# Moving the operand sums of a second matrix product between the blocks of an interleaved schedule

## The chip, the cores and the metric

One core of a Trainium2 chip runs the whole program. The metric is the device time of one execution in microseconds (us). The kernel before was run three times: 297.32, 300.2 and 303.18 us, median 300.2. Changes of about 2% are the smallest that a comparison here is meant to tell from none.

## The reference, cut to what matters

A linear attention (softmax over the head dimension of q, softmax over the sequence of k, then two small products) is followed by a two-layer network with SiLU. Its output has 4608 rows, and nearly all of the arithmetic is in the two layers:

```python
kv = np.einsum('bhsd,bhse->bhde', k_s, v)
attn = np.einsum('bhsd,bhde->bhse', q_s, kv)      # 8 batches, 8 heads, 576 rows, 64 wide
x = attn.transpose(0, 2, 1, 3).reshape(4608, 512)
h = x @ w_in                                       # 512 -> 2048
g = h * (1.0 / (1.0 + np.exp(-h)))
out = g @ w_out                                    # 2048 -> 512, float32
```

## The kernel before, in words

The 4608 rows are cut into nine chunks of 512 (chunk 0 to chunk 8). For each chunk the kernel needs its slice of the attention output (XT, 512 wide, transposed), the first product with W1 and SiLU (result GT, two buffers GT0 and GT1 that chunks use in turn), and the second product with W2.

From chunk 1 on, the second product is done in the manner of Strassen and Winograd: the 2048x512 weight W2 and the chunk's GT are cut into two by two blocks, and seven block products P1 to P7 replace eight. The price is sums on VectorE (DVE). On the weight side there are T1 to T4, made once (`t_op`, line 439; T3 is written over a quarter of W2, T4 has two halves). On the data side there are S1 to S4, made for every chunk (`s_op`, line 429): S1 = GT01 + GT11, S2 = S1 - GT00, S3 = GT00 - GT01, which is written in place over GT01, and S4 = GT10 - S2. P5 uses S1 and T1, P6 uses S2 and T2, P7 uses S3 and T3, P4 uses T4, and P3 uses S4. P1 and P2 need no sum. Half of the first product is done in the same way (`group`, lines 344 to 382, matmuls on line 357; its sums on line 320 are called XS here); the other half is plain (`mm1`, matmuls on line 274).

The order of the work is written out by hand. The list `units` holds small blocks of work, and `plan(u, f)` puts extra work in front of unit u. All instructions are issued in that order, each engine runs its own in order, and engines wait for each other through semaphores. `begin[t]` is the first unit of chunk t. For t = 2 to 7 a chunk has 29 blocks: 15 that alternate a plain first-product matmul group of chunk t (`p`) with half of a block product of chunk t-1 (`b`), and then 14 that mix the seven Strassen groups of chunk t (`g`) with the remaining halves (`b`). The products come in the order 1, 2, 6, 5, 7, 4, 3, two halves each:

```python
mix = "pbpbpbpbpbpbpbp", "ggbgbgbgbbgbgb"
```

So P7 begins in block 19, P4 in block 23 and P3 in block 26. In chunk 8 the two parts stand the other way round: there P7 begins in block 17, P4 in block 21 and P3 in block 25.

PSUM sets the coupling around the change. Banks 0 to 3 hold the plain groups `p` in turn. Each is emptied by two instructions: ScalarE (ACT) takes the tanh (line 246, into one of three buffers sg), then DVE multiplies (line 247, scalar_tensor_tensor, into GT). The first two Strassen groups, g1 and g2 in blocks 15 and 16, take over banks 0, 1 and banks 2, 3. So the matmuls of g1 and g2 can't start before DVE has emptied these banks of the last `p` groups. From chunk 3 on the eighth `p` is in bank 0; in chunk 2 it is in bank 2, with the sixth in bank 0 and the seventh in bank 1.

Besides, DVE adds up rows of the exponentials of q for the next batch (line 144) and takes their reciprocals (line 148); GpSimd (POOL) scales the exponentials with these (line 153) and casts v (line 91, into vaug); kv (line 185) and the attention product (line 224) follow in the second part of a chunk. DVE also combines the Strassen results (line 336 for the first product, lines 475 and 486 for the output tiles ow). In chunk 7 and 8 no batch is left to prepare, and POOL has nothing of this to do.

Of the kernel before, what the change touches and what calls it, by code (L numbers as in the profile page):

```python
# [17 lines left out]
def kernel(  # L18
# [9 lines left out]
    nc = tc.nc  # L28
# [257 lines left out]
    def mm1(t, fb):  # L286
        bank = hb[0] % hb[1]
        hb[0] += 1
        mm1_mm(t, fb, bank, range(NC))
        mm1_silu(t, fb, bank)  # L290
# [22 lines left out]
    def xs_op(t, i):  # L313
        in0, in1 = {
            1: (xb(t, 0, 1), xb(t, 0, 0)),
            2: (xb(t, 1, 1), XS4[0]),
            3: (xb(t, 1, 1), xb(t, 0, 1)),
            4: (xb(t, 1, 0), XS4[1]),
        }[i]
        nc.vector.tensor_tensor(out=XS4[i - 1], in0=in0, in1=in1, op=ALU.subtract)  # L320
# [23 lines left out]
    def group(t, i):  # L344
        bank = 0 if i in (1, 6, 7, 4) else 2
        a, bb = {
            1: (wa(0, F0), xb(t, 0, 0)),
            2: (wa(1, F0), xb(t, 1, 0)),
            3: (WS[3], xb(t, 1, 1)),
            4: (wa(1, F1), XS4[3]),  # L350
            5: (WS[0], XS4[0]),
            6: (WS[1], XS4[1]),
            7: (WS[2], XS4[2]),
        }[i]
        for p in range(4):
            for c in range(2):
                nc.tensor.matmul(  # L357
                    out=PS[:, bank + p // 2, (p % 2) * HT:(p % 2 + 1) * HT],
                    lhsT=a[:, c, p * 128:(p + 1) * 128],
                    rhs=bb[:, c, :],  # L360
                    start=(i in (1, 2, 5) and c == 0 and p % 2 == 0),
                    stop=(i in (2, 3, 4) and c == 1 and p % 2 == 1),
                    skip_group_check=True,
                )
        if i == 1:
            group_snap(0)
        elif i == 2:
            group_add(0)
        elif i == 6:
            group_snap(1)  # L370
            group_silu(t, 0, F0, 0)
        elif i == 7:
            group_snap(2)
            group_add(2)
        elif i == 4:
            group_silu(t, None, F1, 0)
        elif i == 3:
            group_silu(t, 2, F1, 1)
            group_add(1)
            group_silu(t, 1, F0, 1)  # L380
# [36 lines left out]
    def blk(t, kh, th):  # L417
        return GTS[t % 2][:, kh * HF:(kh + 1) * HF, th * HT:(th + 1) * HT]

    def s_op(t, i, f0=0, f1=HF):  # L420
        in0, in1, op = {
            1: (blk(t, 0, 1), blk(t, 1, 1), ALU.add),
            2: (SS[1], blk(t, 0, 0), ALU.subtract),
            3: (blk(t, 0, 0), blk(t, 0, 1), ALU.subtract),
            4: (blk(t, 1, 0), SS[2], ALU.subtract),
        }[i]
        f = slice(f0, f1)
        o = blk(t, 0, 1) if i == 3 else SS[i]
        nc.vector.tensor_tensor(out=o[:, f], in0=in0[:, f], in1=in1[:, f], op=op)  # L429

    def t_op(i, eng, f0=0, f1=HF):
        o, in0, in1 = {
            1: (T1, B12, B11),
            2: (T2, B22, T1),
            3: (T3, B22, B12),
            4: (T4, B21, T2),
        }[i]
        f = slice(f0, f1)
        eng.tensor_tensor(out=o[:, f], in0=in0[:, f], in1=in1[:, f], op=ALU.subtract)
# [160 lines left out]
    def plan(u, f):  # L600
        at.setdefault(u, []).append(f)
# [7 lines left out]
    begin = {1: len(units)}  # L609
# [6 lines left out]
    def b_units(t, order):  # L616
        got = []
        for i in order:
            got.append(lambda t=t, i=i: prod(t, i, 0))

            def second(t=t, i=i):
                prod(t, i, 1)
                after(t, i)

            got.append(second)
        return got
# [8 lines left out]
    for t in range(2, NCH):  # L635
        begin[t] = len(units)
        bs = b_units(t - 1, ORDER)
        ps_ = [lambda t=t, fb=fb: mm1(t, fb) for fb in (0, 8, 1, 9, 2, 10, 3, 11)]
        gs = [lambda t=t, i=i: group(t, i) for i in (1, 2, 6, 5, 7, 4, 3)]
        plan(begin[t] + 2, lambda t=t: s_op(t - 1, 1))  # L640
        plan(begin[t] + 4, lambda t=t: s_op(t - 1, 2))
        plan(begin[t] + 11, lambda t=t: s_op(t - 1, 3))
        plan(begin[t] + 16, lambda t=t: s_op(t - 1, 4))
        mix = "pbpbpbpbpbpbpbp", "ggbgbgbgbbgbgb"
        for x in "".join(mix) if t < NCH - 1 else "ggbgbgbgbbgbgb" + "pbpbpbpbpbpbpbp":
            units.append({"p": ps_, "b": bs, "g": gs}[x].pop(0))
        assert not (ps_ or bs or gs)
        x = begin[t] + (1 if t < NCH - 1 else 0)
        plan(x, lambda t=t: (xs_op(t, 1), xs_op(t, 2), xs_op(t, 3), xs_op(t, 4)))
# [102 lines left out]
    plan(b1 + 30, lambda: mm2_plain_out(0, (2, 3)))  # L752
    plan(begin[2], lambda: (hb.__setitem__(0, 3), hb.__setitem__(1, 4)))
    plan(begin[3], lambda: hb.__setitem__(0, 1))
    plan(begin[2] + 12, lambda: t_op(3, nc.vector))
    plan(begin[2] + 14, lambda: t_op(4, nc.vector, 0, 4))
    plan(begin[2] + 16, lambda: t_op(4, nc.vector, 4, 8))

    for t in range(2, NCH - 1):
        b = t + 1  # L760
# [58 lines left out]
```

## Time and profile before

| what | value |
|---|---|
| the three timed runs | 297.32, 300.2, 303.18 us |
| the profiled execution | 300.68 us |
| its span, first to last instruction | 298.9 us |
| mean granted TensorE clock | 0.959 |
| TensorE matmuls (PE), busy | 269.3 us (90%) |
| VectorE (DVE), busy | 206.8 us (69%) |
| ScalarE (ACT), busy | 182.4 us (61%) |
| GpSimd (POOL), busy | 72.1 us (24%) |
| HBM read and written | 36.70 MB and 9.44 MB |

How to read the profile: each row of a timeline is a start, a duration, an engine, the line of the kernel, and out<-in with shapes. Brackets give the engine's idle time before it and what ended that. PE is TensorE's matmuls, PEld its weight loads. PEclk is the clock that TensorE was granted, 1.00 being full speed. The first row of the wait view is a sum over all waits of one kind, then their number, then the longest.

### The profile page before, as it was taken

The page shows a single profiled execution, that of the slowest core. Times are in us where ns is not written, and L with a number is a line of the kernel's source. Part 1 is how long each engine was busy: PE and PEld are TensorE (multiplying, and loading weights), DVE is VectorE, ACT ScalarE, POOL GpSimd, SP SyncE. Part 2 cuts the span into 40 slices and gives each one's busy share as a digit, 9 for nine tenths or more (in the row PEclk, how much of TensorE's full clock was granted, in tenths as well). Part 3 has the DMA queues.
Part 4 walks back from the last instruction along what each step waited for, and adds up shares of the span by engine and source line. Part 5 has one row for each costly group of instructions (what it writes and reads, how often), then busy time and mean ns, then how long its engine had stood idle before and what let it go on. Part 6 is the DMA issues. An engine that isn't in the chain of part 4 may idle for free.

```text
span 298.9 us, 6097 instructions
## 1 busy us (share of the span) xinstructions
PE 269.3 (90%) x2540; PEld 189.4 (63%) x2540; DVE 206.8 (69%) x294; ACT 182.4 (61%) x232; POOL 72.1 (24%) x62
## 2 busy tenths in 40 slices
PE   8799999999499986999599977999599989999994
PEld 3377544456277654776387645866387668886783
DVE  3867888789944897259935896459835964666753
ACT  5768748578347891679457871789267446765320
POOL 0936925402800054000900063002700000000002
PEclk9999999999869996999989997999799999999999
DMA  7999996898661567335782479251403300600343
GB/s 263 293 224 346 286 317 261 206 383 269 164 231 29 113 226 196 132 82 138 197 283 58 87 237 232 86 118 24 79 2 77 66 0 2 136 8 3 78 99 105
DMA packets 35500, 45.88 MB, mean 154 GB/s; under 512 B 16208, under 2 KB 20048, under 8 KB 35472
## 3 DMA queue, kind: packets, MB, share of 16 engines
q1 hardware_dynamic: 29568, 33.69, 40.5%
q0 software_dynamic: 5584, 11.54, 14.8%
q8 instruction: 20, 0.33, 0.5%
q10 hardware_dynamic: 320, 0.26, 0.3%
q14 instruction: 8, 0.07, 0.1%
HBM read 36.70 MB, written 9.44 MB: 154 GB/s over the span
## 4 chain that ended last, share of the span: by engine, by line
PE 56%; DVE 23%; ACT 11%; issue 4%; DMA 2%; POOL 1%; SPq 0%; DVEq 0%; ACTq 0%
PE PS L455 22%; PE PS L357 14%; PE PS L274 11%; DVE GT L247 7%; DVE zq L144 4%; DVE GT L429 4%; PE PS L393 3%; PE PS L254 3%; DMA vt<-in_v_dram 2%; DVE ow L475 2%; ACT L342 2%; PE PS L224 2%; ACT GT L342 2%; ACT sg L246 2%; ACT h L333 2%
## 5 line engine op out<-in xcount | busy, mean ns | idle before, releaser
L247 DVE SCALAR_TENSOR_TENSOR GT<-sg,PS 128x512 f16<-128x512 f32 (+2 forms) x88 | 58.1, 675 | 21.8 <-ACT sg L246 21.0
L274 PE MATMUL PS<-XT,W 128*128 128x512 f16 (+1 forms) x288 | 71.2, 373 | 0.3 <-ACT ow L405 0.3
L246 ACT ACTIVATE sg<-PS 128x512 f32<-128x512 f32 (+2 forms) x88 | 51.7, 597 | 28.7 <-PE PS L274 24.3
L153 POOL TENSOR_TENSOR eq<-eq,rzq 128x1152 bf16<-128x1152 bf16 x13 | 27.5, 2117 | 128.0 <-DVE rzq L148 125.6
L455 PEld LDWEIGHTS <-GT 128*128 128x128 f16 x512 | 49.6, 98 | 13.1 <-issue 1.2
L333 ACT COPY h<-PS 128x1024 f32<-128x1024 f32 x21 | 21.2, 1012 | 47.4 <-PE PS L357 47.4
L455 PE MATMUL PS<-W,GT 128*128 128x256 f16 x384 | 49.1, 273 | 0.0
L455 PEld LDWEIGHTS <-S 128*128 128x128 f16 x384 | 38.8, 101 | 10.1
L336 DVE TENSOR_TENSOR h<-PS,h 128x1024 f32<-128x1024 f32 x21 | 25.7, 1225 | 24.6 <-PE PS L357 20.1
L274 PEld LDWEIGHTS <-W 128*128 128x128 f16 x288 | 27.9, 98 | 21.3 <-issue 1.3
L357 PE MATMUL PS<-XT,W 128*128 128x256 f16 x112 | 19.8, 347 | 20.8 <-DVE GT L247 20.8
L357 PEld LDWEIGHTS <-W 128*128 128x128 f16 x168 | 19.0, 113 | 28.0 <-issue 22.6
L455 PE MATMUL PS<-T,S 128*128 128x256 f16 x256 | 35.3, 286 | 0.0
L475 DVE SCALAR_TENSOR_TENSOR ow<-PS,sc 128x512 f32<-128x512 f32 x7 | 4.8, 692 | 28.9 <-ACT sc L471 28.9
L357 PEld LDWEIGHTS <-WS 128*128 128x128 f16 x224 | 21.7, 101 | 4.5 <-issue 1.2
L342 ACT ACTIVATE GT<-h 128x1024 f16<-128x1024 f32 x21 | 22.2, 1058 | 2.1 <-DVE h L336 2.1
L357 PE MATMUL PS<-XS,WS 128*128 128x256 f16 x168 | 22.8, 281 | 0.0
L89 ACT CAST XT<-PS 128x1024 f16<-128x1024 f32 (+2 forms) x18 | 17.4, 964 | 7.7 <-PE PS L224 7.7
L676 POOL DMA_DIRECT2D out_dram<-ow x4 | 2.2, 550 | 77.8 <-DVE ow L661 77.8
L91 POOL CAST vaug<-vt 128x1152 bf16<-128x1152 f32 x12 | 20.4, 1730 | 0.0
L108 ACT ACTIVATE eq<-qt 128x1152 bf16<-128x1152 f32 x16 | 18.6, 1161 | 2.9 <-DMA qt<-in_q_dram 2.8
L111 ACT ACTIVATE ek<-kt 128x1152 bf16<-128x1152 f32 x16 | 18.7, 1170 | 0.7 <-DMA kt<-in_k_dram 0.7
(76 smaller groups left out, 333.3 us busy)
## 6 DMA issues: line engine op xcount, KB each, us to landing
out_dram<-ow SPq DMA_DIRECT2D x64, 128.0 KB, 2.4
qt<-in_q_dram SPq DMA_DIRECT2D x12, 576.0 KB, 4.9
kt<-in_k_dram SPq DMA_DIRECT2D x12, 576.0 KB, 5.6
vt<-in_v_dram SPq DMA_DIRECT2D x12, 576.0 KB, 6.8
qt<-in_q_dram POOLq DMA_DIRECT2D x4, 576.0 KB, 13.0
kt<-in_k_dram POOLq DMA_DIRECT2D x4, 576.0 KB, 13.3
vt<-in_v_dram POOLq DMA_DIRECT2D x4, 576.0 KB, 12.5
W<-in_moe_w_out_dram POOLq DMA_DIRECT2D x4, 512.0 KB, 15.0
```

Source lines behind the costliest of these rows:

```text
L91: eng.tensor_copy(o, i)
L108: nc.scalar.activation(out=half(st[b]["eq"], cc), in_=jgd(b, "qt", cc), func=ACT.Exp)
L111: nc.scalar.activation(out=half(ek, cc), in_=jgd(b, "kt", cc), func=ACT.Exp)
L153: eng.tensor_tensor(out=e, in0=e, in1=r[:, :, :, None].to_broadcast([128, J, 2, D]), op=ALU.mult)
L246: nc.scalar.activation(out=s, in_=i, func=ACT.Tanh, scale=OS)
L247: nc.vector.scalar_tensor_tensor(out=o, in0=s, scalar=1.0, in1=i, op0=ALU.add, op1=ALU.mult)
L274: nc.tensor.matmul(out=PS[:, bank, o0:TCH], lhsT=W1[:, c, fb * 128:(fb + 1) * 128], rhs=XTS[t % 2][:, c, o0:TCH], start=(c == 0), stop=(c ...
L333: nc.scalar.copy(out=H[i], in_=PS[:, 0:2, :].rearrange("p b n -> p (b n)"))
L336: nc.vector.tensor_tensor(out=H[i], in0=PS[:, 2:4, :].rearrange("p b n -> p (b n)"), in1=H[i], op=ALU.add)
L342: nc.scalar.activation(out=group_out(t, f, n), in_=x, func=ACT.Silu, scale=1.0 / XS)
L357: nc.tensor.matmul(out=PS[:, bank + p // 2, (p % 2) * HT:(p % 2 + 1) * HT], lhsT=a[:, c, p * 128:(p + 1) * 128], rhs=bb[:, c, :], start=(i ...
L455: nc.tensor.matmul(out=PS[:, bank, m * HN:(m + 1) * HN], lhsT=a[:, fc, m * 128:(m + 1) * 128], rhs=bb[:, fc, :], start=(first and fc == 0) ...
```

## The change

Five numbers of the plan change. S3 (`s_op(.., 3)`) moves from block 11 of each chunk to block 5, S4 from block 16 to block 21. In chunk 2, T3 moves from block 12 to block 15, and the two halves of T4 from blocks 14 and 16 to blocks 18 and 20. Nothing is added or taken away; PE's, POOL's and the DMA queues' own orders stay the same, and ACT's too.

```diff
-        plan(begin[t] + 11, lambda t=t: s_op(t - 1, 3))
-        plan(begin[t] + 16, lambda t=t: s_op(t - 1, 4))
+        plan(begin[t] + 5, lambda t=t: s_op(t - 1, 3))
+        plan(begin[t] + 21, lambda t=t: s_op(t - 1, 4))
...
-    plan(begin[2] + 12, lambda: t_op(3, nc.vector))
-    plan(begin[2] + 14, lambda: t_op(4, nc.vector, 0, 4))
-    plan(begin[2] + 16, lambda: t_op(4, nc.vector, 4, 8))
+    plan(begin[2] + 15, lambda: t_op(3, nc.vector))
+    plan(begin[2] + 18, lambda: t_op(4, nc.vector, 0, 4))
+    plan(begin[2] + 20, lambda: t_op(4, nc.vector, 4, 8))
```

DVE's order in chunk 3 before, from S2 (S_78<-S_77,..) to the add that combines g1 and g2 (L336). GT_75 is GT0, which P1 to P7 of chunk 2 read; GT_76 is GT1, which the `p` groups fill; the row GT_75<-GT_75 is S3, S_79 is S4:

```order
L429 TENSOR_TENSOR S_78<-S_77,GT_75 128x2048
L247 SCALAR_TENSOR_TENSOR GT_76<-sg,PS 128x512
L144 TENSOR_REDUCE zq<-eq 128x18
L148 RECIPROCAL rzq<-zq 128x18
L247 SCALAR_TENSOR_TENSOR GT_76<-sg,PS 128x512
L475 SCALAR_TENSOR_TENSOR ow<-PS,sa 128x2x256
L144 TENSOR_REDUCE zq<-eq 128x18
L148 RECIPROCAL rzq<-zq 128x18
L247 SCALAR_TENSOR_TENSOR GT_76<-sg,PS 128x512 x2
L429 TENSOR_TENSOR GT_75<-GT_75 128x8x256
L247 SCALAR_TENSOR_TENSOR GT_76<-sg,PS 128x512 x2
L429 TENSOR_TENSOR S_79<-GT_75,S_78 128x2048
```

The same place now:

```order
L429 TENSOR_TENSOR S_78<-S_77,GT_75 128x2048
L247 SCALAR_TENSOR_TENSOR GT_76<-sg,PS 128x512
L429 TENSOR_TENSOR GT_75<-GT_75 128x8x256
L144 TENSOR_REDUCE zq<-eq 128x18
L148 RECIPROCAL rzq<-zq 128x18
L247 SCALAR_TENSOR_TENSOR GT_76<-sg,PS 128x512
L475 SCALAR_TENSOR_TENSOR ow<-PS,sa 128x2x256
L144 TENSOR_REDUCE zq<-eq 128x18
L148 RECIPROCAL rzq<-zq 128x18
L247 SCALAR_TENSOR_TENSOR GT_76<-sg,PS 128x512 x4
L336 TENSOR_TENSOR h_1511<-PS,h_1511 128x1024
L429 TENSOR_TENSOR S_79<-GT_75,S_78 128x2048
```

S3 now stands ahead of both row sums instead of ahead of the last two multiplies, and S4 behind the add of line 336 instead of ahead of it. S3 is still ahead of the last multiply. Chunks 4 to 6 show the same exchange.

DVE's order in chunk 2 before, from the fifth and sixth multiply to the add of line 336 (W_71<-W_71 is T3, T_74 is T4):

```order
L247 SCALAR_TENSOR_TENSOR GT_75<-sg,PS 128x512 x2
L429 TENSOR_TENSOR GT_76<-GT_76 128x8x256
L439 TENSOR_TENSOR W_71<-W_71 128x8x256
L247 SCALAR_TENSOR_TENSOR GT_75<-sg,PS 128x512
L439 TENSOR_TENSOR T_74<-W_71,T_73 128x1024
L247 SCALAR_TENSOR_TENSOR GT_75<-sg,PS 128x512
L429 TENSOR_TENSOR S_79<-GT_76,S_78 128x2048
L439 TENSOR_TENSOR T_74<-W_71,T_73 128x1024
L336 TENSOR_TENSOR h_1122<-PS,h_1122 128x1024
```

The same place now:

```order
L247 SCALAR_TENSOR_TENSOR GT_75<-sg,PS 128x512 x4
L439 TENSOR_TENSOR W_71<-W_71 128x8x256
L336 TENSOR_TENSOR h_1121<-PS,h_1121 128x1024
L439 TENSOR_TENSOR T_74<-W_71,T_73 128x1024 x2
L429 TENSOR_TENSOR S_79<-GT_76,S_78 128x2048
```

The four sums that stood among the last multiplies and ahead of the add are gone from there: S3 went forward to block 5, the others stand behind the last multiply.

## The prediction

> **What bounds the kernel now.** I read the page first, then the waits of TensorE, then the timeline of PE around those waits.
>
> ```profile
> PE 269.3 (90%) x2540; PEld 189.4 (63%) x2540; DVE 206.8 (69%) x294; ACT 182.4 (61%) x232; POOL 72.1 (24%) x62
> ...
> PE PS L357 <- DVE GT L247: 20.8, 7, 4.0
> ```
>
> PE is the busiest engine, and only one kind of wait of its matmuls is large: seven times, 20.8 us in all, the Strassen groups (L357) wait for DVE's multiply (L247), which empties the banks that they need. The timeline shows these seven: two in chunk 2, then one in each of chunks 3 to 7.
>
> ```profile
> 81.36 1.01 PE L357 MATMUL PS<-XT,W 128*128 128x256 f16 x4 [4.04 <-DVE GT L247]
> 82.92 1.87 PE L357 MATMUL PS<-XT,W 128*128 128x256 f16 x8 [0.55 <-DVE GT L247]
> ...
> 114.89 3.57 PE L357 MATMUL PS<-XT,W 128*128 128x256 f16 x16 [3.69 <-DVE GT L247]
> ...
> 148.79 3.26 PE L357 MATMUL PS<-XT,W 128*128 128x256 f16 x16 [3.69 <-DVE GT L247]
> ...
> 181.13 2.48 PE L357 MATMUL PS<-XT,W 128*128 128x256 f16 x16 [3.69 <-DVE GT L247]
> ...
> 213.79 3.19 PE L357 MATMUL PS<-XT,W 128*128 128x256 f16 x16 [3.69 <-DVE GT L247]
> ...
> 243.78 1.91 PE L357 MATMUL PS<-XT,W 128*128 128x256 f16 x16 [1.41 <-DVE GT L247]
> ```
>
> The same 16 matmuls take 1.91 us in chunk 7, after a short wait, and 2.48 to 3.57 us after the long ones. So the wait costs twice: as idle time, and as slow matmuls behind it. The granted clock, asked for in stretches of 3.4 and 6.8 us, shows why:
>
> ```profile
> 79.91:86.74 6.83, 4.83 (x23) 3.25 (x23) 5.92 (x7) 1.01 (x1) 1.82 (x1) 0.50 1.00 303
> ...
> 114.05:120.87 6.82, 5.98 (x29) 4.12 (x29) 4.00 (x4) 1.01 (x1) 1.71 (x2) 0.50 1.00 272
> ...
> 148.18:151.59 3.41, 2.80 (x14) 1.94 (x14) 2.54 (x2) 0.90 (x1) 1.47 (x2) 0.50 1.06 164
> 178.90:182.31 3.41, 1.18 (x11) 1.06 (x11) 3.41 (x4) 0.11 (x1) 3.10 (x2) 1.00 0.76 152
> 182.31:185.73 3.42, 3.42 (x18) 2.44 (x17) 1.98 (x2) 0.91 (x1) 0.00 (x0) 0.50 0.97 246
> ...
> 213.03:216.45 3.42, 2.66 (x13) 1.86 (x13) 2.70 (x3) 0.76 (x1) 1.63 (x2) 0.50 0.81 154
> 240.35:243.77 3.42, 2.02 (x14) 1.18 (x13) 2.37 (x4) 1.25 (x3) 0.00 (x0) 1.00 0.00 0
> ...
> 175.49:178.90 3.41, 1.95 (x13) 1.17 (x12) 3.38 (x5) 2.19 (x4) 2.82 (x3) 1.00 0.79 266
> ```
>
> The first number behind the length is PE's busy time, the last but two is the clock. In each of chunks 2 to 6 the clock falls to 0.50 for 3.41 us or twice that, and the falls lie whole multiples of 3.41 us apart (79.91 to 114.05 is ten), so they follow a fixed raster. A raster window with 1.18 us of PE work was followed by a slow one; windows with 1.95 and 2.02 us were not. At half clock, half of the busy time is lost: 2.4 us in chunk 2, and 3.0, 1.4, 1.7 and 1.3 us, together 7.4 us, in chunks 3 to 6.
>
> What makes the multiply late is in DVE's timeline of chunk 3 (the first five rows); the sixth row is from chunk 7, the last two are POOL's of chunk 3:
>
> ```profile
> 105.28 0.69 DVE L247 SCALAR_TENSOR_TENSOR GT<-sg,PS 128x512 f16<-128x512 f32 x1
> ...
> 107.52 0.63 DVE L247 SCALAR_TENSOR_TENSOR GT<-sg,PS 128x512 f16<-128x512 f32 x1
> ...
> 110.22 1.22 DVE L247 SCALAR_TENSOR_TENSOR GT<-sg,PS 128x512 f16<-128x512 f32 x2
> 111.35 2.29 DVE L429 TENSOR_TENSOR GT<-GT 128x2048 f16<-128x2048 f16 x1
> 113.57 1.27 DVE L247 SCALAR_TENSOR_TENSOR GT<-sg,PS 128x512 f16<-128x512 f32 x2
> ...
> 240.17 1.22 DVE L429 TENSOR_TENSOR GT<-GT 128x2048 f16<-128x2048 f16 x1
> ...
> 107.74 2.12 POOL L153 TENSOR_TENSOR eq<-eq,rzq 128x1152 bf16<-128x1152 bf16 x1 [26.01 <-DVE rzq L148]
> ...
> 110.45 2.12 POOL L153 TENSOR_TENSOR eq<-eq,rzq 128x1152 bf16<-128x1152 bf16 x1 [0.59 <-ACT ek L111]
> ```
>
> None of the rows of chunk 3, nor any between them, has an idle time in brackets: DVE is full from 105.28 on, and the last multiply, which ends at 114.84, lets g1 start at 114.89. S3 takes 2.29 us here because POOL's scaling runs until 112.57; in chunk 7, with POOL idle, the same sum takes 1.22 us.
>
> **The change part by part.**
>
> S3 in chunks 3 to 6. In block 5 it stands behind the multiply of 105.28, still ahead of the last multiply on an engine that is full between them. So moving it frees nothing by the order alone; all work ahead of the last multiply is the same. What is saved is the price: POOL has been idle for 26.01 us until 107.74, since it waits for the reciprocal that now comes behind S3, so S3 should run at 1.22 instead of 2.29 us. That is 1.07 us a chunk, 4.3 us over four chunks, with both ends between 0 (POOL in its way there too) and 1.07. The wait of 3.69 becomes 2.62 us. The row sums and one multiply shift back by 1.1 us: the fourth multiply, which empties bank 0 for the eighth plain group, and POOL's scaling. Both have cover: the eighth group starts at 110.17, that multiply (107.52) ended at 108.15 and would end at 109.3; and what follows POOL is needed late.
>
> ```profile
> 112.51 3.25 POOL L91 CAST vaug<-vt 128x1152 bf16<-128x1152 f32 x2
> ...
> 124.00 0.80 PE L185 MATMUL PS<-vaug,ek 64*64 64x65 bf16 x72
> 125.39 0.69 DVE L475 SCALAR_TENSOR_TENSOR ow<-PS,sc 128x512 f32<-128x512 f32 x1 [5.59 <-ACT sc L471]
> ...
> 110.17 1.03 PE L274 MATMUL PS<-XT,W 128*128 128x512 f16 x4
> ```
>
> The casts end 8.2 us ahead of the product that reads them. With the casts 1.1 us later and PE up to 4 us earlier, 3 us are left.
>
> S4 in chunks 3 to 7. It moves from in front of the add (L336) to behind it, into the 5.59 us in which DVE waits for ACT. Between 1.22 us and the 2.07 us that it took beside the casts it fits; P3 needs it five blocks later. I take nothing for it. If the cover were gone, the output add, the copy of kv and the attention product behind it would wait with it, 1.2 us a chunk or more.
>
> Chunk 2. Here S3, T3 and half of T4 stood among the last multiplies:
>
> ```profile
> 75.20 1.22 DVE L247 SCALAR_TENSOR_TENSOR GT<-sg,PS 128x512 f16<-128x512 f32 x2
> ...
> 76.33 2.29 DVE L429 TENSOR_TENSOR GT<-GT 128x2048 f16<-128x2048 f16 x1
> ...
> 76.72 0.60 PE L357 MATMUL PS<-XT,W 128*128 128x256 f16 x4
> ...
> 77.49 4.24 POOL L91 CAST vaug<-vt 128x1152 bf16<-128x1152 f32 x2
> ...
> 78.55 2.16 DVE L439 TENSOR_TENSOR W<-W 128x2048 f16<-128x2048 f16 x1
> ...
> 82.19 0.67 DVE L247 SCALAR_TENSOR_TENSOR GT<-sg,PS 128x512 f16<-128x512 f32 x1
> ...
> 87.39 1.04 PE L455 MATMUL PS<-W,GT 128*128 128x256 f16 x8
> ```
>
> With S3 ahead at 1.14 us (1.22 less the overlap with its neighbour), the fifth and sixth multiply end at 77.56, the seventh at 78.2, the eighth at 78.8. The first half of g1, which ran at 76.72, now waits 0.9 us, its second half and g2 0.15 us each: 1.2 us of idle time in place of 4.04 + 0.55. That is 3.4 us saved, and with windows this full the clock has no cause to fall: 2.4 us more, together 5.8. Everything up to P7 (87.39) moves to about 81.5. T3 starts at 78.8, right behind the eighth multiply, while POOL casts; T3 took 2.16 us in that company, which would end at 81.0, just ahead of P7. If it had to let both casts pass (3.25 us from about 78.7), it would end at 83.1 and P7 would wait 1.6 us. I take 0, since one of the two casts was let through in the old row, and keep 1.6 for the range. The Trainium skill speaks against this spot: SBUF — State Buffer, section SBUF: two separate sides, says that a VectorE operation with two SBUF inputs and a GpSimd operation exclude each other for a whole instruction. The trace agrees (2.29 against 1.22 us); by that rule T3 would start at the first cast's end, some 80.3, and end near 81.4, and the sum stays.
>
> Chunks 7 and 8. In chunk 7 the wait of 1.41 us is for the tanh of the last group, not for a full DVE, and S3 costs 1.22 us already: nothing. In chunk 8 PE has no wait; S4 now ends some 0.5 us ahead of P3 there, by the same 1.2 us durations: nothing.
>
> The clock in chunks 3 to 6. An idle stretch of 2.62 us is new. The limit lies between 1.4 and 2.2 us of idle time in one window of 3.41 (1.95 and 1.18 us busy, above). If 2.62 us fall anywhere on the raster, more than 1.4 us of them lie in one window in 9 cases of 10, more than 2.2 in 4 to 5 of 10; I take two thirds to three quarters. So three of four chunks still fall, each for one window at 1.4 us lost (the three single ones lost 1.3 to 1.7): 4.2 us in place of 7.4, a saving of 3.2, between 0 and 7.4.
>
> Sum: 5.8 + 4.3 + 3.2 = 13.3 us. Against the profiled execution of 300.7 us (span 298.9) this gives **287.4 us**; the median of the three runs, 300.2, is the same within their spread.
>
> **The rivals.**
>
> The clock falls in all four chunks as before. The idle stretch stays longer than 2.2 us, which speaks for it. Then 5.8 + 4.3 = 10.1: 290.6 us.
>
> The clock falls in none. Then 5.8 + 4.3 + 7.4 = 17.5: 283.2 us. For it: a wait shorter than one window can never leave a whole window empty. Against it: the window before 182.31 held 1.18 us of work and the clock still fell. The Trainium skill has this rule (TensorE: Matmul & The Clock Gate, section What's actually happening: back to half clock after at least one idle window of about 3.4 us); the trace agrees with the length of the window but not with the need for a wholly idle one.
>
> S3 is still in POOL's way. Then chunks 3 to 6 keep their wait of 3.69 and their clock, and chunk 2 gains 4.7 instead of 5.8 us: 296.0 us, within 2%. Against it: the 26.01 us in which POOL has nothing to run.
>
> Slower: S4 takes the place of the wait. It stands ahead of the output add, the kv copy and the attention product on DVE. If it ended behind the 5.59 us of cover, PE would wait for the attention product; only from 2.7 us beyond the cover in each of five chunks is the gain of 13.3 us used up, and at twice that (5.4 us) the time is 300.7 - 13.3 + 27.0 = 314.4. Against it: the longest S4 in the trace took 2.07 us.
>
> **How the numbers follow.** Forecast, some of the four falls left: 0.5. All falls left: 0.18. None left: 0.17. S3 in POOL's way, or T3 holding P7 on top: 0.1. Slower: 0.02; the rest is spread. The range reaches from 283 (no fall left) to 292.5 (all falls left, and P7 waiting 1.6 us). Faster by over 2% (below 294.2; about 2% is also what a measurement of this kernel can tell from no change): 0.9; within 2%: 0.08; slower: 0.02.
>
> **What would show each step.** Right: the wait of L357 for L247 at about 2.6 us in chunks 3 to 6, under 1 us apiece in chunk 2, and still 1.41 in chunk 7; S3 (GT<-GT) at 1.22 us throughout; stretches at clock 0.50 fewer or shorter; P7, P4 and P3 without a wait. Wrong: S3 still at 2.29 us; the wait gone from L357 but back at L455 (for T3, T4 or S4) or at the attention product; a wait of 2.6 us with all the slow windows as before (then the first rival), or with none (then the second).

## The result and the profile after

The changed kernel takes 286.42 us (median of four runs, 285.22 to 286.89); the kernel before takes 300.69 us beside it (297.32 to 303.18). The ratio is 0.9555, with a 95% interval of 0.9466 to 0.9644: faster. Between the medians it is 14.3 us; the ratio leaves out the kernel before's run of 303.18 us, which is over 1.5% above that kernel's fastest, and stands for some 13.4 us. The forecast was 287.4 us, a gain of 13.3. The profiled execution took 286.77 us, with a span of 285.0 us against 298.9.

The page of the kernel after, its engines, and then the longest of its waits on PE:

```profile
PE 264.4 (93%) x2539; PEld 186.7 (66%) x2540; DVE 197.5 (69%) x294; ACT 182.4 (64%) x232; POOL 66.6 (23%) x62
...
PE PS L357 <- DVE GT L247: 10.1, 6, 2.0
PE PS L455 <- DVE ow L475: 1.9, 4, 0.5
```

The wait of the Strassen groups for the multiply has halved, from 20.8 to 10.1 us. A second wait is new: four times, some half a microsecond, a block product (L455) waits for the output add (L475). PE's busy time fell by 4.9 us though it does the same matmuls, since fewer of them ran at half clock. The same places in PE's timeline as before, chunks 2 to 7:

```profile
76.11 1.03 PE L274 MATMUL PS<-XT,W 128*128 128x512 f16 x4
77.85 2.23 PE L357 MATMUL PS<-XT,W 128*128 128x256 f16 x16 [0.71 <-DVE GT L247]
...
81.67 1.04 PE L455 MATMUL PS<-W,GT 128*128 128x256 f16 x8
...
102.72 1.03 PE L274 MATMUL PS<-XT,W 128*128 128x512 f16 x4
104.21 1.03 PE L455 MATMUL PS<-T,S 128*128 128x256 f16 x8 [0.47 <-DVE ow L475]
105.08 1.03 PE L274 MATMUL PS<-XT,W 128*128 128x512 f16 x4
108.10 3.57 PE L357 MATMUL PS<-XT,W 128*128 128x256 f16 x16 [1.99 <-DVE GT L247]
...
139.68 1.91 PE L357 MATMUL PS<-XT,W 128*128 128x256 f16 x16 [1.99 <-DVE GT L247]
...
169.61 1.91 PE L357 MATMUL PS<-XT,W 128*128 128x256 f16 x16 [1.99 <-DVE GT L247]
...
199.53 2.88 PE L357 MATMUL PS<-XT,W 128*128 128x256 f16 x16 [2.00 <-DVE GT L247]
...
229.91 1.91 PE L357 MATMUL PS<-XT,W 128*128 128x256 f16 x16 [1.41 <-DVE GT L247]
```

Chunk 2 has one wait of 0.71 us left of 4.04 + 0.55, and P7 (81.67) follows without one. In chunks 3 to 6 the wait is 1.99 to 2.00 us, and twice of four times the 16 matmuls behind it run at full speed (1.91 us). Chunk 7 is as it was. The clock around three of these waits, in windows of the raster (PE's busy time is the first number behind the length, the clock the last but two):

```profile
104.71:108.12 3.41, 1.42 (x10) 0.74 (x9) 3.30 (x6) 1.01 (x2) 2.82 (x3) 1.00 0.53 166
108.12:111.53 3.41, 3.41 (x17) 2.35 (x17) 0.00 (x0) 1.01 (x1) 2.05 (x2) 0.50 0.76 144
166.15:169.56 3.41, 1.46 (x10) 0.78 (x8) 3.37 (x6) 1.08 (x2) 2.82 (x3) 1.00 0.52 178
196.87:200.28 3.41, 1.42 (x11) 0.87 (x9) 2.60 (x5) 0.60 (x1) 2.99 (x2) 1.00 0.00 0
200.28:203.69 3.41, 3.41 (x18) 2.35 (x16) 1.17 (x2) 1.01 (x1) 1.32 (x2) 0.50 0.90 173
```

The clock fell in chunks 3 and 6 and in no other: with 1.42 us of work in a window it fell, with 1.46 us (chunk 5) it did not. DVE in chunk 3 of the kernel after, from S3 on, and POOL beside it:

```profile
100.17 1.22 DVE L429 TENSOR_TENSOR GT<-GT 128x2048 f16<-128x2048 f16 x1
101.30 1.35 DVE L144 TENSOR_REDUCE zq<-eq 128x18 f32<-128x1152 bf16 x1
102.75 0.27 DVE L148 RECIPROCAL rzq<-zq 128x18 f32<-128x18 f32 x1
102.93 0.63 DVE L247 SCALAR_TENSOR_TENSOR GT<-sg,PS 128x512 f16<-128x512 f32 x1
103.48 0.68 DVE L475 SCALAR_TENSOR_TENSOR ow<-PS,sa 128x512 f32<-128x512 f32 x1
104.07 1.34 DVE L144 TENSOR_REDUCE zq<-eq 128x18 f32<-128x1152 bf16 x1
105.45 0.27 DVE L148 RECIPROCAL rzq<-zq 128x18 f32<-128x18 f32 x1
105.63 2.41 DVE L247 SCALAR_TENSOR_TENSOR GT<-sg,PS 128x512 f16<-128x512 f32 x4
...
112.92 1.22 DVE L429 TENSOR_TENSOR S<-GT,S 128x2048 f16<-128x2048 f16 x1
...
103.15 2.12 POOL L153 TENSOR_TENSOR eq<-eq,rzq 128x1152 bf16<-128x1152 bf16 x1 [21.03 <-ACT sg L246]
```

S3 costs 1.22 us, well ahead of POOL's scaling at 103.15. DVE is still full up to the last multiply, which ends at 108.04, just ahead of g1 at 108.10. And the output add, which empties PSUM bank 5, now ends at 104.16: the first half of P5, which starts that bank anew, waits for it until 104.21. S4 runs in the gap behind the add of g1 and g2, at 1.22 us.

### The profile page after: what moved, and what is told of

Its sections match the earlier page's. It is cut to its first block, busy times and chain, and to the rows that moved or that the text cites. A ratio compares the mean times of both kernels' runs of the same rounds, so it can differ in the third digit from the quotient of the medians.

```text
span 285.0 us, 6096 instructions
## 1 busy us (share of the span) xinstructions
PE 264.4 (93%) x2539; PEld 186.7 (66%) x2540; DVE 197.5 (69%) x294; ACT 182.4 (64%) x232; POOL 66.6 (23%) x62
## 4 chain that ended last, share of the span: by engine, by line
PE 59%; DVE 18%; ACT 10%; DMA 5%; issue 4%; SPq 1%; POOL 1%; DVEq 0%; ACTq 0%
PE PS L455 22%; PE PS L357 14%; PE PS L274 12%; DVE GT L247 7%; PE PS L393 5%; DVE zq L144 4%; PE PS L254 3%; DMA vt<-in_v_dram 3%; DVE ow L475 2%; ACT L342 2%; PE PS L224 2%; ACT GT L342 2%; ACT h L333 2%; DVE GT L429 2%; ACT eq L108 2%
## 5 line engine op out<-in xcount | busy, mean ns | idle before, releaser
L455 PEld LDWEIGHTS <-GT 128*128 128x128 f16 x512 | 49.6, 98 | 13.1 <-issue 1.2
L455 PE MATMUL PS<-W,GT 128*128 128x256 f16 x384 | 49.1, 273 | 0.0
L336 DVE TENSOR_TENSOR h<-PS,h 128x1024 f32<-128x1024 f32 x21 | 25.7, 1224 | 31.4 <-PE PS L357 22.5
L455 PEld LDWEIGHTS <-S 128*128 128x128 f16 x384 | 38.0, 99 | 11.9 <-issue 3.0
L274 PEld LDWEIGHTS <-W 128*128 128x128 f16 x288 | 27.9, 98 | 21.3 <-issue 1.3
L455 PE MATMUL PS<-T,S 128*128 128x256 f16 x256 | 33.4, 276 | 1.9 <-DVE ow L475 1.9
L357 PEld LDWEIGHTS <-W 128*128 128x128 f16 x168 | 17.5, 104 | 15.8 <-issue 12.1
L357 PE MATMUL PS<-XT,W 128*128 128x256 f16 x112 | 16.3, 304 | 10.1 <-DVE GT L247 10.1
L357 PEld LDWEIGHTS <-WS 128*128 128x128 f16 x224 | 21.0, 98 | 3.8 <-issue 1.2
L357 PE MATMUL PS<-XS,WS 128*128 128x256 f16 x168 | 21.8, 273 | 0.0
L144 DVE TENSOR_REDUCE zq<-eq 128x18 f32<-128x1152 bf16 x12 | 16.1, 1345 | 3.9 <-ACT eq L108 3.9
L254 PE MATMUL PS<-XT,W 128*128 128x288 f16 x128 | 16.5, 286 | 0.7 <-DVE GT L247 0.4
## 6 DMA issues: line engine op xcount, KB each, us to landing
kt<-in_k_dram POOLq DMA_DIRECT2D x4, 576.0 KB, 13.3
```

What stands on the lines that cost most here:

```text
L144: nc.vector.reduce_sum(out=z, in_=e, axis=AX.X)
L254: nc.tensor.matmul(out=PS[:, 2 * (fb % 3) + n, 0:S // 2], lhsT=W1[:, c, fb * 128:(fb + 1) * 128], rhs=XTS[0][:, c, n * (S // 2):(n + 1) * ...
L274: nc.tensor.matmul(out=PS[:, bank, o0:TCH], lhsT=W1[:, c, fb * 128:(fb + 1) * 128], rhs=XTS[t % 2][:, c, o0:TCH], start=(c == 0), stop=(c ...
L336: nc.vector.tensor_tensor(out=H[i], in0=PS[:, 2:4, :].rearrange("p b n -> p (b n)"), in1=H[i], op=ALU.add)
L357: nc.tensor.matmul(out=PS[:, bank + p // 2, (p % 2) * HT:(p % 2 + 1) * HT], lhsT=a[:, c, p * 128:(p + 1) * 128], rhs=bb[:, c, :], start=(i ...
L455: nc.tensor.matmul(out=PS[:, bank, m * HN:(m + 1) * HN], lhsT=a[:, fc, m * 128:(m + 1) * 128], rhs=bb[:, fc, :], start=(first and fc == 0) ...
```

## The experiments

The theory is the one on record: S3 gained by getting out of POOL's way, chunk 2 by clearing the last multiplies, and the clock by the shorter idle time. The rivals were that one move needs another, that the place in DVE's order counts and not POOL, and that the slow matmuls have another cause than the idle time.

**S3 alone.** The kernel before, with the one line:

```diff
-        plan(begin[t] + 11, lambda t=t: s_op(t - 1, 3))
+        plan(begin[t] + 5, lambda t=t: s_op(t - 1, 3))
```

> The kernel before with only S3 moved (block 11 to 5). Theory: S3 is worth what it costs less without GpSimd's scaling beside it, in chunks 3 to 6, with the clock that follows; in chunk 2 T3 and half of T4 still stand among the last multiplies. So S3 at 1.22 us everywhere, the wait of the Strassen groups at about 2 us in chunks 3 to 6 with a new wait of 0.47 us for the output add, and in chunk 2 still over 3 us: about 291.5 us. Rival (the changed times need all three moves together, since S4 blocks what S3 gives): near 300.

Measured: 291.25 us, ratio 0.9666 (0.9564 to 0.9768). The wait of chunks 3 to 6 is 1.99 us with 0.46 to 0.47 us at the output add, S3 takes 1.22 us; in chunk 2 the waits are 0.71, 2.21 and 0.96 us. Chunk 3 of this run, DVE and PE:

```profile
104.45 1.22 DVE L429 TENSOR_TENSOR GT<-GT 128x2048 f16<-128x2048 f16 x1
...
108.49 1.03 PE L455 MATMUL PS<-T,S 128*128 128x256 f16 x8 [0.47 <-DVE ow L475]
...
112.38 1.91 PE L357 MATMUL PS<-XT,W 128*128 128x256 f16 x16 [1.99 <-DVE GT L247]
```

S3 needs no other move.

**S4 alone.**

```diff
-        plan(begin[t] + 16, lambda t=t: s_op(t - 1, 4))
+        plan(begin[t] + 21, lambda t=t: s_op(t - 1, 4))
```

> The kernel before with only S4 moved (block 16 to 21). Theory: S4 stood behind the last multiply already, so no wait of TensorE depended on it; it fills a gap of VectorE in its new place: 300.7 us, within 1 us. Rival (S4 held back the add behind it, and with it ScalarE's SiLU): 3 us or more faster. S4 at 1.22 us in place of up to 2.07 us by either.

Measured: 301.48 us beside 301.18, ratio 0.9989 (0.9927 to 1.005). The move of S4 is worth nothing that can be seen, though it makes S4 itself shorter: it was off the chain in both places.

**T3 and T4 alone.** The three lines of chunk 2 of the change, S3 and S4 left in blocks 11 and 16.

> The kernel before with only T3 and T4 moved (chunk 2). Theory: S3 stays ahead of the seventh multiply at 2.2 us, T3 and half of T4 no longer do, so the waits of chunk 2 fall from 4.6 to 2 to 3 us and nothing changes in chunks 3 to 6: 297 to 298.5 us, depending on whether the clock still falls in chunk 2. Rival (T3 now holds P7): no faster than 300, with a wait at the block products.

Measured: 296.16 us, ratio 0.9844 (0.9741 to 0.9946), a little better than expected. PE's only wait in chunk 2 of this run is one of 1.95 us, and the clock fell there for one window instead of two. By the ratios the three parts alone gained 3.3%, 0.1% and 1.6%, 5.0% in all; together they gained 4.5%. They add up as far as can be told, since the interval of each is about 1% to either side.

**The clock by itself.** Filler matmuls in front of g1, `heat(n, bank)` being the kernel's own warm-up helper; bank 6 is free there:

```diff
+    for t in range(2, NCH - 1):
+        plan(begin[t] + 15, lambda: heat(16, 6))
```

> The kernel before with 16 matmuls on a zero tile into PSUM bank 6 in front of the first Strassen group of chunks 2 to 7 (3.5 us at full clock, results thrown away), so that TensorE is not idle while it waits for VectorE's multiply. Theory: the multiply comes no earlier and the Strassen groups start when they did, but the clock does not fall any more, which is worth 2.4 us in chunk 2 and 7.4 us in chunks 3 to 6, less about 2 us in chunk 7, where the filler is longer than the wait: 292 to 294 us. Rival (the slow matmuls behind the wait have another cause than the idle time): 300.7 us or more.

Measured: 293.97 us, ratio 0.9794 (0.9715 to 0.9872). Chunk 3 of this run, PE:

```profile
110.30 1.03 PE L274 MATMUL PS<-XT,W 128*128 128x512 f16 x4
111.16 3.62 PE L529 MATMUL PS<-warm 128*128 128x512 bf16 x16
115.02 1.91 PE L357 MATMUL PS<-XT,W 128*128 128x256 f16 x16 [0.24 <-DVE GT L247]
```

From the eighth plain group to g1 it is 4.72 us, as before (110.17 to 114.89). But g1 and g2 now take 1.91 us instead of 3.57, and the granted clock is 1.00 over the whole span. So the slow matmuls came from the idle time. Filling it gained about 7 us, although the filler is too long for chunk 7: from the eighth plain group to g1 it is 4.32 us there instead of 2.43. So the slow matmuls cost the kernel before about 9 us.

**S3 under POOL's scaling.** The changed kernel with one number more:

```diff
-        plan(begin[t] + 5, lambda t=t: s_op(t - 1, 3))
+        plan(begin[t] + 8, lambda t=t: s_op(t - 1, 3))
```

> The changed kernel with S3 in block 8 instead of 5 (behind the output add, ahead of the second row sum). Theory: there GpSimd's first scaling runs beside it, so S3 costs about 2 us or more again and the wait of the Strassen groups goes back to about 3.5 us in chunks 3 to 6, while the wait for the output add (0.47 us) is gone, since that add stands ahead of S3; the clock falls more often: 290 to 294 us. Rival (what counted was taking S3 away from the last multiplies, wherever it goes): 286.4 us or less, as the wait for the output add is gone.

Measured: 295.2 us, ratio 0.9816 (0.9778 to 0.9854): slower than the changed kernel by 8.8 us and a little above the expected range, as the clock fell in all of chunks 2 to 6. DVE and POOL in chunk 3 of this run, and then g1:

```profile
105.62 2.28 DVE L429 TENSOR_TENSOR GT<-GT 128x2048 f16<-128x2048 f16 x1
...
104.70 2.12 POOL L153 TENSOR_TENSOR eq<-eq,rzq 128x1152 bf16<-128x1152 bf16 x1 [21.56 <-DVE rzq L148]
...
111.85 3.24 PE L357 MATMUL PS<-XT,W 128*128 128x256 f16 x16 [3.68 <-DVE GT L247]
```

S3 is away from the last multiplies here too, but POOL's scaling runs until 106.82, S3 takes 2.28 us, and the wait is back at 3.68 us. As long as S3 stands ahead of the last multiply, what counts in chunks 3 to 6 is not which multiplies it is ahead of, but what it costs.

**The kernel before without POOL's scaling.** In chunks 2 to 6 GpSimd's scaling of q's exponentials is left out, so q's softmax is not normalised there; S3 stays in block 11:

```diff
-                pl(x + 1 + i, lambda i=i, b=b: (qsum(b, i), qnorm(b, i, nc.gpsimd)))
+                pl(x + 1 + i, lambda i=i, b=b: qsum(b, i))
```

> The kernel before with GpSimd's scaling of the exponentials of q left out in chunks 2 to 6 (the rows of q's softmax stay unnormalised there), so that nothing runs on GpSimd beside S3 in block 11. Theory: S3 costs 1.22 us in its old place, and the wait of the Strassen groups falls by 1.07 us in chunks 3 to 6 as it did with the move; in chunk 2 S3 and T3 cost 1.2 us each instead of 2.2; with the clock that follows 288 to 293 us. Rival (the place in the order was what counted): S3 at 1.22 us perhaps, but the wait still near 3.69 us and 300 us.

Measured: 292.76 us, ratio 0.9726 (0.9681 to 0.9771). Chunk 3, DVE and then PE:

```profile
111.14 1.22 DVE L429 TENSOR_TENSOR GT<-GT 128x2048 f16<-128x2048 f16 x1
112.28 1.28 DVE L247 SCALAR_TENSOR_TENSOR GT<-sg,PS 128x512 f16<-128x512 f32 x2
...
113.61 3.08 PE L357 MATMUL PS<-XT,W 128*128 128x256 f16 x16 [2.62 <-DVE GT L247]
```

In its old place, with POOL quiet, S3 costs 1.22 us, and the wait is the 2.62 us that the prediction worked out for the move. Per chunk that is the same gain without the move. The casts of v went from S3's neighbourhood too (the next one starts at 122.11), so this run shows that POOL's work is the cause; it does not tell its instructions apart.

**S3 behind the last multiply.** The changed kernel with:

```diff
-        plan(begin[t] + 5, lambda t=t: s_op(t - 1, 3))
+        plan(begin[t] + (16 if 2 < t < NCH - 1 else 5), lambda t=t: s_op(t - 1, 3))
```

> The changed kernel with S3 in block 16 of chunks 3 to 7 (behind the last multiply, ahead of the add of g1 and g2; chunks 2 and 8 keep block 5). Theory: VectorE is full up to the last multiply, so taking S3 out from ahead of it frees its whole 1.13 us: the wait for the output add is gone, the Strassen groups wait 1.4 to 1.5 us for tanh and multiply, the clock never falls; S3 runs beside GpSimd's casts at 1.2 to 2.3 us in time that VectorE waits anyway, and P7 does not wait for it. 278 to 280 us. Rival (the scaled price was all there was to gain, the rest of the wait is ScalarE's): 285 to 287 us.

Measured: 278.94 us, ratio 0.9271 (0.9244 to 0.9298). Chunk 3, DVE, POOL and PE:

```profile
104.74 2.41 DVE L247 SCALAR_TENSOR_TENSOR GT<-sg,PS 128x512 f16<-128x512 f32 x4
107.07 2.19 DVE L429 TENSOR_TENSOR GT<-GT 128x2048 f16<-128x2048 f16 x1
109.32 1.23 DVE L336 TENSOR_TENSOR h<-PS,h 128x1024 f32<-128x1024 f32 x1
...
107.03 3.25 POOL L91 CAST vaug<-vt 128x1152 bf16<-128x1152 f32 x2
...
107.21 1.91 PE L357 MATMUL PS<-XT,W 128*128 128x256 f16 x16 [1.48 <-DVE GT L247]
```

S3 is slow again beside POOL's casts (2.19 us), and it costs nothing: it stands behind the last multiply. The wait is 1.48 us, the wait for the output add is gone, and the clock fell nowhere ahead of the tail. This was the part of S3 that the change left on the chain. Four times 1.13 us and the two falls of the clock that are gone (1.7 us each, below) make 7.9 us; against the changed kernel's median it is 7.5.

**The banks.** The changed kernel, with g1's banks freed by the fifth and sixth plain groups:

```diff
-    plan(begin[3], lambda: hb.__setitem__(0, 1))
+    plan(begin[3], lambda: hb.__setitem__(0, 0))
```

> The changed kernel with the plain groups' PSUM banks counted from 0 instead of 1 from chunk 3 on, so that the sixth plain group, not the eighth, is the last one in the banks of g1; the eighth stands in bank 3 and only g2 needs it. Theory: g1 starts 1.2 us earlier, behind the sixth multiply, and fills 0.9 us of the wait ahead of g2; the idle stretch before g1 falls below 1 us, a second one of about 0.3 us comes before g2, the clock does not fall: 279 to 281 us. Rival (the banks do not matter since g2 waits for the same multiply): 285 to 287 us.

Measured: 278.19 us, ratio 0.9249 (0.9224 to 0.9275), a little better than expected. In chunks 3 to 6 g1 waits 0.21 us, and g1 and g2 together take 2.38 us instead of 1.91: the rest of the wait lies between them. The output add still costs its 0.46 to 0.47 us.

**Filler matmuls in the changed kernel.** As above, with 9 in place of 16.

> The changed kernel with 9 matmuls on a zero tile into PSUM bank 6 in front of the first Strassen group of chunks 2 to 7 (1.9 us at full clock, results thrown away). Theory: the wait for the multiply stays as long but is filled, and the clock falls in no chunk, which is worth the two falls of 1.6 to 1.7 us that the changed kernel's profile shows, less about 0.5 us in chunk 7 and up to 1 us in chunk 2, where the filler is longer than the wait: 283 to 285 us. Rival (the slow stretches in the changed kernel do not come from the idle time): 286.4 us or more.

Measured: 285.13 us, ratio 0.951 (0.9385 to 0.9636), 0.1 above the expected range; against the changed kernel's 286.42 the difference is smaller than the intervals. The clock is 1.00 throughout and the wait of L357 is gone from the list, but this run's span is that of the changed kernel (284.9). It came to the eighth plain group of chunk 2 at 78.26 instead of 76.11, ahead of any filler; 0.8 us of that is a wait for W1's load. From there to the end it took 206.6 instead of 208.9 us. So the two falls fit a worth of 2 to 3 us, but the times do not show it by themselves.

**Both edits that helped.** S3 in block 16 and the banks from 0:

> The changed kernel with both edits that helped: S3 in block 16 of chunks 3 to 7 and the plain groups' banks counted from 0. Theory: g1 no longer waits at all, g2 waits some 0.5 us for tanh and multiply of the eighth plain group, the output add is not late; against the banks alone (about 1.1 us of idle time a chunk) half a microsecond a chunk is left to gain: 275.5 to 277 us. Rival (behind the multiplies another limit is reached, such as ScalarE or the wait of P7 for S3): 278 us or more.

Measured: 273.8 us (273.34 to 274.26), ratio 0.9143 (0.9049 to 0.9236), better than expected and the best of all. Chunk 3, PE:

```profile
103.96 1.04 PE L455 MATMUL PS<-T,S 128*128 128x256 f16 x8
104.83 1.03 PE L274 MATMUL PS<-XT,W 128*128 128x512 f16 x4
105.70 2.24 PE L357 MATMUL PS<-XT,W 128*128 128x256 f16 x16
```

No wait stands ahead of any of the three; 0.33 us is left inside g1 and g2 (2.24 against 1.91).

## Why the prediction was right

**S3 in chunks 3 to 6: 4.3 us, measured 4.3.** The price was right (1.22 for 2.29 us), and so was its cause, which two runs show from both sides: beside POOL in another block it is 2.28 us, in the old block without POOL 1.22. The wait was to become 2.62 us; it became 0.47 + 1.99 = 2.46 us in two places. By starts: in the kernel before, g1 began 4.72 us behind the eighth plain group (110.17 to 114.89), where 0.87 us is the pace of an unhindered group, so it lost 3.85. After, P5 began 1.49 us behind the seventh (102.72 to 104.21) and g1 3.02 us behind the eighth (105.08 to 108.10), so they lost 0.62 and 2.15, together 2.77. Per chunk 1.08 us was gained, against 1.07 forecast; chunks 4 to 6 give the same by their starts.

What the prediction did not see is the place of the first loss. It checked whether the late multiply would hold up the eighth plain group and found cover, but not the output add, the next instruction on DVE, which P5's bank waits for. This cost nothing more here because DVE is full to the last multiply: what PE loses at P5 it does not lose again at g1.

**Chunk 2: 5.8 us, measured 6.0.** P7 moved from 87.39 to 81.67, and the chunk's eighth plain group stood 0.25 us later (75.86 to 76.11), which makes 5.97. The idle time that was to be left, 1.2 us, is 0.87 us ahead of g1 (76.11 to 77.85, less the pace) and 0.32 within g1 and g2 (2.23 against 1.91). T3 went beside the casts and did not hold P7:

```profile
78.92 2.19 DVE L439 TENSOR_TENSOR W<-W 128x2048 f16<-128x2048 f16 x1
...
78.87 3.25 POOL L91 CAST vaug<-vt 128x1152 bf16<-128x1152 f32 x2
```

It took 2.19 us and ended at 81.11, ahead of P7. The prediction put the first cast's end at some 80.3, half of their 3.25 us behind 78.7, and T3's, had T3 to let that cast pass, near 81.4. But the first cast takes 1.16 us and the second, which runs into T3, 2.16: the first ended at 80.03, and T3 1.08 us behind it. The casts end at 82.12, ahead of the product that reads them (84.38).

**The clock: 3.2 us, measured 4.0.** Three falls of 1.4 us lost were expected in chunks 3 to 6, two of 1.7 us came (3.41 us of work at half clock each): the number and the size were both off, and the errors partly cancel, which is luck. So is the number of falls itself, which hangs on where the raster stands in an execution. The profiled execution with its two falls has a mean clock of 0.988; the four timed ones have 0.985 to 0.994, and the one with 0.994, which fits one fall fewer, is the fastest at 285.22 us. The estimate of the limit, between 1.4 and 2.2 us of idle time in a window, holds the measured one: 1.42 us of work, 1.99 idle, fell; 1.46, 1.95 idle, did not. The rival that the clock would fall nowhere, which needs a wholly idle window, is out: the windows that tripped it were 42% busy.

**Chunks 7 and 8, S4: nothing, measured nothing.** The wait of chunk 7 is 1.41 us in both kernels, and S4 alone is 0.9989.

The terms as measured, 6.0 + 4.3 + 4.0, less the 0.25 us of the late start, make 14.0 us; the span fell by 13.9. The rival of S3 still in POOL's way (296.0) is the kernel with S3 in block 8, which measured 295.2. What the prediction rightly said of the order, that moving S3 ahead on a full engine frees nothing by itself, also points at what was left, though the prediction does not draw it: the remaining 1.13 us per chunk of S3 ahead of the last multiply, which block 16 took out.

## What to carry to other kernels

On an engine that is full up to the instruction that others wait for, moving work earlier gains only what the work gets cheaper there; moving it behind that instruction gains all of it, even when it gets dearer, as long as nothing waits for it there. Look at which other engine runs beside an operation before choosing its place, and at every buffer that the delayed instructions behind it free, not only at the first. Where a short idle stretch of TensorE decides whether its clock falls, a wait may cost a third to four fifths more than its length (in the kernel before 3.69 us of idle time, and 1.3 to 3.0 us lost to slow matmuls behind it).

## What the runs showed of the hardware

The clock's limit was sharper than expected. It goes by windows of 3.41 us, on a raster fixed for the whole execution. Of the windows at full clock in the twelve profiles, all with 1.42 us of PE work or less were followed by a half-clock window; from 1.45 us on none was, except for two in chunk 2 (1.47 us with T3 and T4 alone moved, 1.65 us with S3 in block 8), and why these fell stays open. The way back asks for more: a half-clock window with 2.61 us of work or less was followed by another one, from 2.65 us on by full clock. This is why a fall lasted one window after some waits and two after others. Matmuls on a tile of zeros were enough to keep the clock up: 1.00 over the whole span of both profiles with fillers. A sum of two f16 tiles that DVE began while GpSimd was at work ended about 1.08 us behind the end of GpSimd's instruction (S3 in chunk 3 before, 113.64 behind 112.56; T3, 81.11 behind 80.03), close to the 1.22 us that it takes alone. And a wait inside a stream of matmuls costs about 0.15 us more than the idle time in its brackets: 0.47 us delayed P5 by 0.62 us. The profile shows a group of matmuls as 1.03 us long where the next one starts 0.87 us behind it.
